# Squared-ReLU attention and a gated feed-forward layer: the third batch's keys and queries by DMA transposes, with four feed-forward units in front of its attention

## The chip, the core and the metric

The kernel runs on one core of a Trainium2 chip. The metric is the device time of one execution in microseconds (us). Three runs of the kernel before gave 439.3, 439.08 and 439.69 us, median 439.3 us.

The engines are called as the profile calls them: PE (TensorE, matmuls), with its weight loads as PEld; DVE (VectorE); ACT (ScalarE); POOL (GpSimd), which here issues the loads; and SP (SyncE), which here issues the stores and the DMA transposes. SPq is SP's queue of DMA issues.

## The reference

There are 8 batches of 448 tokens with 12 heads of 64 columns (768 columns in all). The attention has no softmax. The feed-forward layer has 1536 hidden columns.

```python
def _attn_ref(q, k, v):                        # each (8, 12, 448, 64)
    scale = 1.0 / np.sqrt(q.shape[-1])
    scores = scale * np.matmul(q, k.transpose(0, 1, 3, 2))
    attn = np.maximum(scores, 0.0) ** 2 / S
    return np.matmul(attn, v)

def _moe_ref(x, w_gate, w_val, w_out):         # x is the attention's output as (3584, 768)
    gate = np.maximum(x @ w_gate, 0.0)
    val = x @ w_val
    return gate * val @ w_out
```

Inputs and output are float32. The kernel computes in bf16, sums in float32, and applies all the scales at the end, when it copies the output from PSUM.

## The kernel before, in words

**Order.** Every instruction is pinned, so each engine runs its own instructions in the order in which the code issues them, and waits in place for what the others have not finished. Batches are numbered b = 0 to 7. Batch 0 has its own loop (`first_batch`). Batches 1 to 7 run in `batch(b)`, which goes through n = 0 to 7. At each n it issues three score or value tiles (`burst`), then ACT's ReLU (line 166) and DVE's square (line 170) of the scores, and one or two "gaps". A gap takes units of the feed-forward layer of the batch before from the list `ffn` and issues them. So while batch b's attention runs, batch b - 1's feed-forward layer fills PE.

**Units.** A `gv_unit` makes one 128-row block of the gate and of the value product: 12 matmuls each, an ACT ReLU for the gate, and a DVE multiplication into `hT` (line 244). An `out_unit` makes 384 output columns for 128 tokens with 24 matmuls, and an ACT copy (line 267); the second half's unit issues two stores of 192 KB on SP (line 275). Batches come in pairs: an even batch brings 12 gv units and 6 out units, an odd one 12 and 8. `start_gaps` spreads the units that are left in `ffn` evenly over the gaps of a batch.

**Keys and queries.** Scores need keys and queries with the head's 64 columns on the partitions (`operands`, line 142). There are two ways. For batches below `PE_B` (line 126), `transposes` makes 16 PE transposes for one pair of heads into a PSUM tile `kq_ps` (line 159), and DVE copies it to `kq_sb` (line 161). These run in the middle of a unit (`midway`), one pair of heads at a time, and the next batch's first pair is made at n = 6. From `PE_B` on, `dma_transposes(b)` is called at n = 2 of the batch before: DVE copies the keys into `kr` and the queries into `qr`, regrouped (line 136), and SP issues four DMA transposes for `kT` and four for `qT` (line 139). Each of the four covers a quarter of the tokens for all heads, so the first score tile of a batch needs the first `kT` transpose and all four `qT` transposes. `kr` and `qr` exist once.

**Loads.** POOL issues `kn`, `qn` and `vn` (line 90), two DMAs each, for batch b + 1 at n = 0 of batch b. There are two buffers of each, so a load waits until the last reader of the buffer is done, and all loads behind it on POOL wait too. The readers of `kn` and `qn` are PE's transposes in one way and DVE's regrouping copies in the other. `low_values(b)` (line 108) is a small DVE copy inside `vn`, needed before batch b's first value tile at n = 2. It is issued at n = 5 of the batch before, and for batch 1 at that batch's head.

**Value tiles.** Every eighth tile of a batch is a value tile: `av_last` opens it in the burst, `av_rest` closes it after the first gap, and DVE copies it into `xT` (line 416). Three of these copies complete `xT` of a batch, at n = 2, 5 and 7, and the batch's feed-forward units read it.

Of the kernel before, what the change touches and what calls it, by code (L numbers as in the profile page):

```python
# [16 lines left out]
def kernel(  # L17
# [17 lines left out]
    B, H, S, D = q.shape  # L35
# [24 lines left out]
    def pin(ins):  # L60
        return tc.keep_in_program_order(ins)
# [36 lines left out]
    def load_qk(b, h0=0, h1=H):  # L98
        load_nat(kn_b[b % NB], k, b, h0, h1)
        load_nat(qn_b[b % NB], q, b, h0, h1)  # L100

    def load_v(b):
        load_nat(v_b[b % NB], v, b, 0, H)

    def low_values(b):

        t = v_b[b % NB].rearrange("p (q s h) i d -> p q s h i d", s=2, h=2)
        pin(nc.vector.tensor_copy(t[64:128, :, 1, :, 3, :], t[0:64, :, 1, :, 3, :]))
# [14 lines left out]
            dma_in(wo_sb[c], rows.rearrange("(kf p) m -> p kf m", p=128))  # L123


    PE_B = 3
    kr = const.tile([128, 4, d_model], BF16, name="kr")
    qr = const.tile([128, 4, d_model], BF16, name="qr")
    kT_b = [const.tile([128, HP, 512], BF16, name=f"kT{i}") for i in range(NB)]
# [1 line left out]
    def dma_transposes(b):  # L131

        n = b % NB
        for nat, grp, tr in ((kn_b[n], kr, kT_b[n]), (qn_b[n], qr, qT_b[n])):
            o = grp.rearrange("p i (h d) -> p i h d", d=D)
            pin(nc.vector.tensor_copy(o, nat.rearrange("p h i d -> p i h d")))
            for i in range(4):
                r = 128 if i < 3 else 64
                pin(nc.sync.dma_start_transpose(out=tr[:, :, i * 128:i * 128 + r], in_=grp[0:r, i, :]))


    def operands(b, hp):

        if b >= PE_B:
            n = b % NB
# [23 lines left out]
    def square_part(dst, r):  # L169
        pin(nc.vector.tensor_tensor(dst, r, r, ALU.mult))  # L170

    def relu2(src, dst, n):
        square_part(dst, relu_part(src, n))
# [25 lines left out]
    def av_rest(b, qd, attn, banks):  # L199
        for c in range(2):  # L200
            for i in range(3):
                for h2, o in HALVES:
                    mm(banks[c][o, :], v_b[b % NB][:, 4 * qd + 2 * c + h2, i, :], attn[:, 8 * c + 2 * i + h2, :], False, i == 2)
# [16 lines left out]
    def flush_relu():  # L220
        while late:
            src, dst, n = late.pop(0)
            late_squares.append((dst, relu_part(src, n)))

    def flush():
        flush_relu()
        while late_squares:
            square_part(*late_squares.pop(0))
# [50 lines left out]
    def ffn_units(b):  # L279
        b0 = b - b % 2  # L280
        if b == b0:
            hT_of[b0] = hpool.tile([128, KF, 2 * S], BF16, name="hT")
        hT, xT = hT_of[b0], xT_of[b]
        units = [lambda mf=mf: gv_unit(b, mf, xT, hT) for mf in range(KF)]
        for t in (range(0, 3) if b == b0 else range(3, 7)):
            cuts = [0, OH, OH + OH // 2, d_model] if b == B - 1 and t == 6 else [0, OH, d_model]
            for c0, c1 in zip(cuts, cuts[1:]):
                units.append(lambda t=t, c0=c0, c1=c1: out_unit(b0, t, c0, c1, hT, o_state))
        return units


    ffn = []
    share = [0, 0, 0]

    def start_gaps(of):
        share[:] = [len(ffn), of, 0]

    def gap():

        n, of, i = share  # L300
        for _ in range((i + 1) * n // of - i * n // of):
            ffn.pop(0)()
        flush()
        share[2] = i + 1
# [22 lines left out]
    def transpose_pair(b, hp):  # L327
        kqs[b, hp] = operands(b, hp)

    def attn_of(b, qd):  # L330
        if (b, qd) not in attns:
            attns[b, qd] = atpool.tile([128, 14, S], BF16, name="attn")
        return attns[b, qd]

    def burst(b, tiles):

        todo, begun = [], None
        for qd, kind, c, i in tiles:
            attn = attn_of(b, qd)
            if kind == "pair":  # L340
                todo.append(scores(kqs[b, 2 * qd + c], i, attn, 8 * c + 2 * i))
            elif kind == "last":
                todo.append(scores_last((kqs[b, 2 * qd], kqs[b, 2 * qd + 1]), attn))
            else:
                ps = sc_tile()
                banks = [ps[:, c, :S] for c in range(2)]
                av_last(b, qd, attn, banks)
                begun = (qd, banks, ps[:, :, :S])
        return todo, begun

    def first_batch():
        banks = [av_bank(), av_bank()]
        idle_matmuls(banks[0], 14)
        transpose_pair(0, 0)
        idle_matmuls(banks[0], 4)
        av_at = {4: 0, 5: 1, 6: 2}
        for n in range(len(tiles_first) // 3):
            todo, _ = burst(0, tiles_first[3 * n:3 * n + 3])
            if n in av_at:
                av_last(0, av_at[n], attn_of(0, av_at[n]), banks)  # L360
            relu2(*todo[0])
            if n not in av_at:
                idle_matmuls(banks[0], 2)
            if n + 1 < HP:
                transpose_pair(0, n + 1)
            if n not in av_at:
                idle_matmuls(banks[0], 1)
            relu2(*todo[1])
            relu2(*todo[2])
            if n == 3:  # L370
                low_values(0)
            if n in av_at:
                qd = av_at[n]
                av_rest(0, qd, attn_of(0, qd), banks)
                for c in range(2):
                    x = xT_of[0][:, 2 * qd + c, :]
                    if (qd, c) == (NQ - 1, 0):
                        pin(nc.scalar.activation(x, banks[c], AF.Copy))
                    else:
                        pin(nc.vector.tensor_copy(x, banks[c]))  # L380
                banks = [av_bank(), av_bank()] if qd + 1 < NQ else None
# [3 lines left out]
    PAIR_AT = {0: 1, 1: 2, 2: 3, 3: 4, 5: 5, 6: 6}  # L385

    def batch(b):
        if b == 1:
            low_values(1)
        gaps = [(1, 1)] * 8  # L390
        if b == 1:
            gaps = [(0, 1), (1, 1), (1, 1), (0, 1), (0, 1), (0, 1), (0, 1), (1, 1)]
        elif b == 2:
            gaps[5] = (0, 2)
        start_gaps(sum(map(sum, gaps)))
        pending = None
        for n in range(len(tiles_later) // 3):
            todo, begun = burst(b, tiles_later[3 * n:3 * n + 3])
            relu2(*todo[0])
            relu2(*todo[1])  # L400
            late.extend(todo[2:])
            if n == 0 and b < B - 1:
                load_qk(b + 1)
                load_v(b + 1)
            if n in PAIR_AT:
                hp = PAIR_AT[n]
                if hp < HP:
                    midway.append(lambda hp=hp: transpose_pair(b, hp))
                elif b + 1 < B:
                    midway.append(lambda: transpose_pair(b + 1, 0))  # L410
            for _ in range(gaps[n][0]):
                gap()
            if begun:
                qd, banks, both = begun
                av_rest(b, qd, attn_of(b, qd), banks)
                pin(nc.vector.tensor_copy(xT_of[b][:, 2 * qd:2 * qd + 2, :], both))  # L416
            if b + 1 < B and n == 2 and b + 1 >= PE_B:
                dma_transposes(b + 1)
            if b + 1 < B and n == 5:
                low_values(b + 1)  # L420
            for _ in range(gaps[n][1]):
                gap()

    for b in range(B):
        xT_of[b] = xpool.tile([128, KD, S], BF16, name="xT")
        if b == 0:
            first_batch()
        else:
            batch(b)
        if b + 1 < B:  # L430
            ffn.extend(ffn_units(b))
            if b == 0:
                for _ in range(6):
                    ffn.pop(0)()
                midway.append(lambda: transpose_pair(1, 0))
                ffn.pop(0)()
    flush()
    while ffn:
        ffn.pop(0)()
# [31 lines left out]
```

## Time and profile before

| What | Value |
|---|---|
| Median of three runs | 439.3 us |
| The profiled execution's own time | 438.88 us |
| Its span in the trace | 437.0 us |
| PE busy | 425.9 us, 97% of the span |
| DVE, ACT, POOL busy | 210.3, 217.3, 51.9 us |
| Granted PE clock | 1.00 |
| Moved by DMA | 42.22 MB, mean 97 GB/s |

The page has these parts: busy time of each engine; the span in 40 slices with the busy tenths, the DMA share and GB/s; the DMA queues; the chain of work that ended last; groups of instructions with their mean duration and the idle time before them; and DMA issues with the time to landing. The trace behind it gives single instructions in order of time. Batch b's attention begins with its first burst; these stand at 45.93 us for batch 1, 82.94 for batch 2, 137.92 for batch 3, 186.76 for batch 4, 239.51 for batch 5, 288.56 for batch 6 and 341.31 for batch 7.

The loads of a batch are 384 + 288 KB each for keys, queries and values in the units of the page. A DMA share above 1 means that the 16 DMA engines had more than one packet under way.

### The profile page before, as it was taken

Reading aid. Unit: us, or ns where it says so; the run is one execution under the profiler, and the core shown is the slowest. Engines: PE = TensorE matmul, PEld = TensorE weight load, DVE = VectorE, ACT = ScalarE, POOL = GpSimd, SP = SyncE. Lnnn points to the kernel's source line nnn. Section 1 sums busy time; section 2 is a strip of 40 time slices with the busy share of each in tenths; the row PEclk is TensorE's granted clock in tenths of the full one; section 3 lists DMA queues with packets and bytes.
Section 4 is the critical chain, followed back from the end, with each engine's and each line's share of the span. In section 5 each row is a group of like instructions: output and inputs, shape, how many; then the busy total and the mean of one; then the engine's idle time right before and its main releaser. Section 6 shows DMA issues by size and latency. Waiting matters only on the chain.

```text
span 437.0 us, 11447 instructions
## 1 busy us (share of the span) xinstructions
PE 425.9 (97%) x5076; PEld 251.2 (57%) x5076; DVE 210.3 (48%) x332; ACT 217.3 (50%) x323; POOL 51.9 (12%) x75
## 2 busy tenths in 40 slices
PE   7889999999999999999999999999999999999996
PEld 3447655556566555655566555655566555566664
DVE  3872766547534565345533575435653354522210
ACT  3952647554545544564544655545455645532221
POOL 8624302100024000120003000010000000000001
PEclk9999999999999999999999999999999999999999
DMA  9999999912299951393715923170323200030014
GB/s 107 187 204 195 203 205 202 185 40 63 66 152 164 149 84 45 77 190 41 121 38 102 198 65 67 38 137 1 83 47 87 60 2 1 6 102 4 1 38 108
DMA packets 80081, 42.22 MB, mean 97 GB/s; under 512 B 48640, under 2 KB 76544, under 8 KB 80032
## 3 DMA queue, kind: packets, MB, share of 16 engines
q0 software_dynamic: 47232, 23.70, 41.4%
q1 hardware_dynamic: 32720, 17.75, 16.7%
q8 instruction: 39, 0.64, 0.6%
q14 instruction: 10, 0.08, 0.1%
q10 hardware_dynamic: 80, 0.05, 0.0%
HBM read 47.19 MB, written 11.01 MB: 133 GB/s over the span
## 4 chain that ended last, share of the span: by engine, by line
PE 88%; DMA 6%; DVE 3%; ACT 2%; issue 1%; POOL 1%; POOLq 0%; DVEq 0%; ACTq 0%
PE g_ps L64 25%; PE v_ps L64 24%; PE o_ps L64 24%; PE sc_ps L64 13%; DMA vn<-in_v_dram 5%; PE kq_ps L159 1%; ACT r_sb L166 1%; DVE attn L170 1%; DMA qn<-in_q_dram 1%; DVE kq_sb L161 1%; PE xT_ps L64 0%; POOL kn L90 0%; DVE xT L380 0%; DVE hT L244 0%; POOL qn L90 0%
## 5 line engine op out<-in xcount | busy, mean ns | idle before, releaser
L166 ACT ACTIVATE r_sb<-sc_ps 128x896 bf16<-128x896 f32 x168 | 145.3, 922 | 42.3 <-PE sc_ps L64 42.3
L170 DVE TENSOR_TENSOR attn<-r_sb 128x896 bf16<-128x896 bf16 x168 | 104.2, 623 | 91.1 <-ACT r_sb L166 91.0
L64 PE MATMUL g_ps<-xT,wg 128*64 128x448 bf16 x1152 | 126.0, 354 | 0.0
L64 PE MATMUL v_ps<-xT,wv 128*64 128x448 bf16 x1152 | 125.2, 352 | 0.0
L64 PE MATMUL o_ps<-wo,hT 128*64 128x384 bf16 (+1 forms) x1368 | 115.8, 324 | 0.0
L244 DVE TENSOR_TENSOR hT<-v_ps,g_sb 128x448 bf16<-128x448 f32 x96 | 59.9, 624 | 93.4 <-PE v_ps L64 93.4
L238 ACT ACTIVATE g_sb<-g_ps 128x448 bf16<-128x448 f32 x96 | 52.3, 545 | 92.7 <-PE g_ps L64 92.7
L64 PEld LDWEIGHTS <-hT 128*64 128x64 bf16 x1368 | 75.1, 110 | 37.6 <-issue 6.4
L64 PEld LDWEIGHTS <-wg 128*64 128x64 bf16 x1152 | 63.4, 110 | 49.9 <-issue 12.9
L64 PEld LDWEIGHTS <-wv 128*64 128x64 bf16 x1152 | 66.3, 110 | 41.2 <-issue 0.3
L267 ACT ACTIVATE o_sb<-o_ps 128x384 f32<-128x384 f32 (+1 forms) x57 | 27.9, 489 | 80.5 <-PE o_ps L64 80.5
L64 PE MATMUL sc_ps<-attn,vn 128*64 128x448 bf16 (+1 forms) x336 | 35.1, 354 | 0.0
L90 POOL DMA_DIRECT2D vn<-in_v_dram x16 | 12.1, 769 | 160.3 <-PE sc_ps L64 154.6
L416 DVE CAST xT<-sc_ps 128x896 bf16<-128x896 f32 x21 | 22.9, 1091 | 14.3 <-PE sc_ps L64 14.3
L64 PEld LDWEIGHTS <-vn 128*64 128x64 bf16 (+1 forms) x384 | 19.3, 109 | 18.0 <-issue 5.4
L64 PE MATMUL sc_ps<-qT,kT 64*64 64x448 bf16 x420 | 28.4, 357 | 0.0
L90 POOL DMA_DIRECT2D kn<-in_k_dram x20 | 14.6, 745 | 60.5 <-PE kq_ps L159 55.7
L64 PE MATMUL sc_ps<-kq_sb 64*64 64x448 bf16 x252 | 18.0, 358 | 2.5 <-ACT r_sb L166 1.2
L275 POOL DMA_DIRECT2D out_dram<-o_sb x2 | 1.1, 554 | 146.2 <-ACT o_sb L267 146.2
L64 PEld LDWEIGHTS <-kT 64*64 64x64 bf16 x420 | 9.6, 105 | 14.3 <-issue 11.7
L90 POOL DMA_DIRECT2D qn<-in_q_dram x20 | 14.5, 753 | 4.9 <-DMA wv<-in_moe_w_val_dram 2.2
L161 DVE COPY kq_sb<-kq_ps 128x960 bf16<-128x960 bf16 x18 | 11.8, 654 | 6.3 <-PE kq_ps L159 5.8
(26 smaller groups left out, 81.3 us busy)
## 6 DMA issues: line engine op xcount, KB each, us to landing
out_dram<-o_sb SPq DMA_DIRECT2D x54, 192.0 KB, 2.7
vn<-in_v_dram POOLq DMA_DIRECT2D x8, 384.0 KB, 6.0
kn<-in_k_dram POOLq DMA_DIRECT2D x7, 384.0 KB, 9.0
qn<-in_q_dram POOLq DMA_DIRECT2D x7, 384.0 KB, 11.7
vn<-in_v_dram POOLq DMA_DIRECT2D x8, 288.0 KB, 7.6
wo<-in_moe_w_out_dram POOLq DMA_DIRECT2D x2, 1152.0 KB, 20.9
kn<-in_k_dram POOLq DMA_DIRECT2D x7, 288.0 KB, 10.5
qn<-in_q_dram POOLq DMA_DIRECT2D x7, 288.0 KB, 12.6
```

Source lines behind the costliest of these rows:

```text
L64: pin(nc.tensor.matmul(o, lhsT=l, rhs=r, start=start, stop=stop, skip_group_check=True))
L90: pin(nc.gpsimd.dma_start(out=o, in_=i))
L159: pin(nc.tensor.transpose(o, t[:, 2 * hp + h2, i, :], ident))
L161: pin(nc.vector.tensor_copy(kq, ps[:, 0:512 + S]))
L166: pin(nc.scalar.activation(r, src, AF.Relu))
L170: pin(nc.vector.tensor_tensor(dst, r, r, ALU.mult))
L238: pin(nc.scalar.activation(g_sb, g_ps, AF.Relu))
L244: pin(nc.vector.tensor_tensor(hT[:, mf, col:col + S], v_ps, g_sb, ALU.mult))
L267: pin(nc.scalar.activation(out=o_sb[:, c0:c1], in_=o_ps, func=AF.Copy, scale=float(out_scale)))
L275: pin(e.dma_start(out=segment_rows(b0, 2 * t + s)[:, m], in_=o_sb[s * 64:s * 64 + 64, m]))
L416: pin(nc.vector.tensor_copy(xT_of[b][:, 2 * qd:2 * qd + 2, :], both))
```

## The change

`PE_B` goes from 3 to 2, so batch 2 (the third) takes its keys and queries from DMA transposes, and no PE transposes are made for it. The regrouping copies and the eight transposes for batch 2 are issued at n = 7 of batch 1, after the last `xT` copy and before the last gap, and not at n = 2 as for the later batches. `low_values(b)` moves into batch b itself, at n = 1, for all batches from 1 on. After batch 1 four units of its own feed-forward layer, all gv units, are issued ahead of batch 2's first burst; the 16 units that are left then fall on batch 2's 16 gaps, where 20 did before. The extra gap at n = 5 of batch 2 becomes an ordinary one (the number of gaps is 16 in both).

```diff
-    PE_B = 3
+    PE_B = 2
...
     def batch(b):
-        if b == 1:
-            low_values(1)
         gaps = [(1, 1)] * 8
         if b == 1:
             gaps = [(0, 1), (1, 1), (1, 1), (0, 1), (0, 1), (0, 1), (0, 1), (1, 1)]
-        elif b == 2:
-            gaps[5] = (0, 2)
         start_gaps(sum(map(sum, gaps)))
...
             late.extend(todo[2:])
+            if n == 1:
+                low_values(b)
             if n == 0 and b < B - 1:
                 load_qk(b + 1)
                 load_v(b + 1)
...
-            if b + 1 < B and n == 2 and b + 1 >= PE_B:
+            if b + 1 < B and n == (7 if b == 1 else 2):
                 dma_transposes(b + 1)
-            if b + 1 < B and n == 5:
-                low_values(b + 1)
             for _ in range(gaps[n][1]):
                 gap()
...
                 midway.append(lambda: transpose_pair(1, 0))
                 ffn.pop(0)()
+            if b == 1:
+                for _ in range(4):
+                    ffn.pop(0)()
     flush()
```

## The prediction

> **What bounds the kernel now.** I read the page first: busy times, then the chain that ended last.
>
> ```profile
> span 437.0 us, 11447 instructions
> PE 425.9 (97%) x5076; PEld 251.2 (57%) x5076; DVE 210.3 (48%) x332; ACT 217.3 (50%) x323; POOL 51.9 (12%) x75
> PE 88%; DMA 6%; DVE 3%; ACT 2%; issue 1%; POOL 1%; POOLq 0%; DVEq 0%; ACTq 0%
> ```
>
> PE is the bound in every stage after the start, and it runs in order: PE work taken away shortens the end by its own length, and a PE wait lengthens it by its own. So I looked next at PE's waits after 46 us. There is one of any size, and the timeline shows it in batch 1 at n = 6:
>
> ```profile
> 72.50 0.56 PE L64 MATMUL sc_ps<-kq_sb 64*64 64x448 bf16 x5
> 73.05 0.28 DVE L108 COPY vn<-vn 64x384 bf16<-64x384 bf16 x1 [0.88 <-DMA vn<-in_v_dram]
> 73.36 0.66 DVE L161 COPY kq_sb<-kq_ps 128x960 bf16<-128x960 bf16 x1
> 74.08 0.57 PE L64 MATMUL sc_ps<-kq_sb 64*64 64x448 bf16 x7 [1.01 <-DVE kq_sb L161]
> ```
>
> DVE stood at `low_values(2)` until batch 2's values had landed; the copy that PE needed was queued behind it.
>
> Then the place to which the transposes move, and how they run today for batch 3:
>
> ```profile
> 81.10 1.09 DVE L416 CAST xT<-sc_ps 128x896 bf16<-128x896 f32 x1 [1.13 <-PE sc_ps L64]
> 81.38 1.50 POOL L90 DMA_DIRECT2D vn<-in_v_dram  x2 [6.72 <-PE sc_ps L64]
> 82.94 0.76 PE L64 MATMUL sc_ps<-kq_sb 64*64 64x448 bf16 x12
> ...
> 102.59 0.95 DVE L136 COPY kr<-kn 128x3072 bf16<-128x3072 bf16 x1
> 103.57 5.27 SPq L139 DMA_TRANSPOSE kT<-kr  x4
> 108.95 5.18 SPq L139 DMA_TRANSPOSE qT<-qr  x4
> ...
> 120.68 1.50 POOL L90 DMA_DIRECT2D kn<-in_k_dram  x2 [37.81 <-PE kq_ps L159]
> ```
>
> The 82.94 line is batch 2's first burst. Batch 3's transposes were issued from 103.57 to 114.13 us and were needed only at 137.92. The last line is the load of batch 4's keys: POOL was held until batch 2's PE transposes had read the buffer.
>
> **Removed: PE transposes of batch 2.** Six pairs of heads. Batches 2, 4 and 6 each hold 20 units and the same bursts; batch 2 lasts 82.94 to 137.92 = 54.98 us, batches 4 and 6 last 52.75 (186.76 to 239.51, 288.56 to 341.31). The 2.23 us are five pairs (the first is made in batch 1), 0.446 each. Six: **-2.7 us**, all on PE. The six DVE copies of 0.65 us go too; DVE is off the path.
>
> **Moved: `low_values`.** Without the wait at 72.16 to 73.05 the `kq_sb` copy follows the `xT` copy, ending at 72.16 + 0.66 = 72.8, and PE goes on at about 72.9 instead of 74.08: **-1.2 us**. At n = 1 of batch 2 the values have long landed (73.0). In the other batches its 0.28 us waited for nothing, before the move and after.
>
> **Added: regrouping and the wait.** I follow the clock of the trace of before. PE reaches the end of batch 1 earlier by 1.2 and one pair of transposes (0.45), so the `xT` copy ends at 82.19 - 1.65 = 80.5, the `kr` copy (0.95) at 81.5, `qr` at 82.4. The next DVE work is the first gv unit's product, about 83.6, so the copies cost PE nothing; uncovered they would cost 1.9. SP's first transpose is issued at 81.5. Quiet, from first issue to last landing (last issue plus 2.6) the five batches took 11.9, 12.8, 12.7, 12.3 and 13.0 us. Median 12.7: landing at 94.2; best, 93.4.
>
> PE comes to the place of the old burst at 82.94 - 1.65 = 81.3. Four gv units at 2.27 us (first gate matmuls at 31.73 and 34.01 in the row of units at the start) carry it to 90.4. The units are only moved, so they add no work. The first burst needs all of `qT` and waits in order with nothing behind it that PE could take: **+3.8 us even if the transposes run as quietly as today**, +3.0 at the best pace. That alone eats the 3.9 gained.
>
> **But they do not run quietly.** Today no load is under way beside a transpose. In the new place, `vn` for batch 3 is issued at about 79.7, and batch 4's `kn` and `qn`, which waited until 120.68, now wait only for the regrouping copies: issued from 81.5 to about 85. That is 2.0 MB. Nothing shows transposes beside loads, so I bound it. Nearest row: the stores, which go through the same queue, alone and beside just such a group of six loads:
>
> ```profile
> out_dram<-o_sb SPq DMA_DIRECT2D x2, 192.0 KB, 2.6
> ...
> qn<-in_q_dram POOLq DMA_DIRECT2D x1, 384.0 KB, 11.7
> out_dram<-o_sb SPq DMA_DIRECT2D x2, 192.0 KB, 6.3
> ```
>
> (The first from 225 to 227 us, the others from 186 to 200.) A store beside loads lands 3.7 us later. And the work itself, in the table of stretches (columns: stretch, its length, each engine's busy time, clock, DMA share, GB/s):
>
> ```profile
> 104.00:109.00 5.00, 5.00 (x72) 3.05 (x66) 3.92 (x7) 3.46 (x5) 0.00 (x0) 1.00 0.55 123
> 109.00:115.00 6.00, 6.00 (x72) 3.25 (x68) 2.50 (x4) 3.36 (x6) 0.00 (x0) 1.00 0.57 129
> 195.00:199.00 4.00, 4.00 (x46) 2.42 (x44) 1.78 (x3) 1.35 (x3) 0.00 (x0) 1.00 1.33 168
> ```
>
> The eight transposes keep the DMA engines 5 x 0.55 + 6 x 0.57 = 6.2 us. Six loads at the 195 GB/s or so of the loaded slices take 10.3, from 82.2 on, when the loads before them end: 92.5. If the two shared without any gain from overlap, both end at 98.7. So the last landing lies between 93.4 and 98.7, with another 1 us above for single issues of 2.3 to 2.45 us instead of 1.25, as three batches had. The last transpose is issued at about 92.2 and lands quietly at 94.2 (median pace); with the store's whole 3.7 it would be 97.9, but by then the loads thin out. I take 2.2 of it: 96.4. Wait: **+6.0 us**, ends 3.0 and 9.3.
>
> The Trainium skill bears on this (DMA: Bandwidth & Descriptors, "Queues, rings and completion order"): each DMA engine serves the queues that have work in turn, a packet at a time, so loads and transposes would share and neither would be shut out. By that rule I would estimate a landing of 97.5 and a sum of 444.3 in place of 443.2; the store's 3.7 us agree in sign, and no run here shows the transposes' share.
>
> **PE after the wait.** The wait may cost more than its length. At the start PE came from idle:
>
> ```profile
> 1.16 4.67 PE L64 MATMUL xT_ps<-blank 128*64 128x448 bf16 x28 [1.16 <-DVE blank L74]
> 31.73 1.33 PE L64 MATMUL g_ps<-xT,wg 128*64 128x448 bf16 x12
> ```
>
> Twelve such matmuls take 1.14 from start to start when PE has been busy, so 28 should take 27 x 0.095 + 0.36 = 2.9; they took 4.67, 1.8 more, though the granted clock reads 1.00. After the 1.0 us wait at 73 the next unit shows no loss. So the ends are 0 and 1.8; a wait of 6 us is more like the idle start than like 1.0: **+1.8**.
>
> The Trainium skill has a rule that speaks against this change (TensorE: Matmul & The Clock Gate, "Part 1: The HAM clock gate"): after an idle window of about 3.4 us PE runs at half clock until a busy one has passed. The start's 1.8 us agree with it; no wait in the trace is long enough to show it in mid-run. By the rule the sum is 443.2, by the 1.0 us wait's row 441.4.
>
> **The sum.** -2.7 - 1.2 + 6.0 + 1.8 = +3.9 on 438.88 (span 437.0 and 1.9 around it) = 442.8; the profile is 0.4 below the median, so 443.2 in medians.
>
> Other queues: on SP the eight transposes stand ahead of the two stores of batch 1's last out unit (83.57 today, then about 93); their buffer is one of three and is wanted again late in batch 2. Values for batch 4 still wait on POOL for the end of batch 2. With two units between bursts instead of 2.5, ACT has three ReLUs and two copies, 3 x 0.9 + 2 x 0.5 = 3.7 us, against 4.6 of PE; batch 1 managed with one unit. Zero for these; if that cover failed, a few tenths for each of seven steps.
>
> **Rivals.**
> Cover holds (other side): loads do not disturb the transposes and the pace is the best of five, 11.9. The wait is 3.0, too short to slow PE: -0.9, 438.4. It decides at a landing of 93.4, below which the kernel is faster by more than 0.2% (0.9 us, about what a measurement here can tell). For: DMA engines had idle half of the time in the transposes' stretches. Against: four of five paces are slower, and all six loads fall there. 0.07.
> Quiet at the median pace: wait 3.0 to 4.8, 438.4 to 440.2, say 439.2. 0.12.
> PE's clock stays up: as forecast without 1.8: 441.4. For: the granted clock never left 1.00 in any row. Against: the start. 0.22.
> Starved: the loads go first and the transposes end last, 98.7 to 99.7, wait 8.8: 446.0. For: a store's data waited 3.7 us. Against: loaded slices reached 327 GB/s where stores ran beside loads at 190, so the two overlapped. 0.17.
> That the transposes replace nothing is excluded: batch 2's PE transposes are gone from PE's order.
>
> **How the numbers follow.** The forecast, 443.2, has 0.42 (its own range 441.5 to 445). Faster 0.07, same 0.12, slower 0.22 + 0.42 + 0.17 = 0.81. Range 439.0 to 446.8: it leaves out the faster case, and the far end of the starved one.
>
> **What would show it.** A PE wait on `qT` before batch 2's first burst, 4 to 8 us, beginning about 90.4; no wait at 73; transposes issued from 81.5 with landings above 4 us each; `kn` and `qn` loads near 82; the first unit after the wait slower than 2.27 us. It is wrong if the burst starts before 93.4, or if a new wait appears inside batch 2.

## The result and the profile after

The changed kernel takes 452.0 us (median of four executions, 450.64 to 452.74) against 439.19 for the kernel before: a ratio of 1.0285, with a 95% interval of 1.0261 to 1.0309. It is 2.9% slower. The forecast was 443.2 us with a range to 446.8. The direction was right; the size was three times too small, and the time lies outside the range.

The page of the changed kernel, its busy times and its chain:

```profile
span 449.9 us, 11267 instructions
PE 425.4 (95%) x4980; PEld 249.4 (55%) x4980; DVE 208.9 (46%) x328; ACT 217.4 (48%) x323; POOL 52.8 (12%) x75
PE 88%; SPq 4%; DVE 3%; DMA 2%; ACT 1%; issue 1%; POOL 1%; POOLq 0%; DVEq 0%; ACTq 0%
```

PE is still the bound, but SP's queue, which was nowhere in the chain before, now holds 4% of it. PE's waits after 46 us (engine, line, what it waited for: total, times, longest) are a single line:

```profile
PE sc_ps L64 <- DMA qT<-qr: 15.2, 1, 15.2
```

The wait in batch 1 on the `kq_sb` copy has gone, as forecast. In its place stands one wait for `qT`, 15.2 us long. The timeline shows what led to it:

```profile
80.42 0.95 DVE L136 COPY kr<-kn 128x3072 bf16<-128x3072 bf16 x1
81.40 10.19 SPq L139 DMA_TRANSPOSE kT<-kr  x4
81.73 1.88 POOL L90 DMA_DIRECT2D kn<-in_k_dram  x2
83.59 1.51 POOL L90 DMA_DIRECT2D qn<-in_q_dram  x2
91.70 10.44 SPq L139 DMA_TRANSPOSE qT<-qr  x4
105.56 1.33 PE L64 MATMUL sc_ps<-qT,kT 64*64 64x448 bf16 x12 [15.16 <-DMA qT<-qr]
106.83 2.31 PE L64 MATMUL g_ps<-xT,wg 128*64 128x448 bf16 x12
108.98 1.30 PE L64 MATMUL v_ps<-xT,wv 128*64 128x448 bf16 x12
```

The start is as forecast: the transposes go out at 81.4 us and the loads of batch 4's keys and queries at 81.7. But four transposes take SP 10.2 and 10.4 us to issue, where they took 5.3 and 5.2. The last issue and what PE waited for stand in the chain (start, us, what):

```profile
94.53 2.88 SPq L139
97.45 2.74 SPq L139
100.24 5.19 DMA qT<-qr
```

The last landed at 105.4 (issue at 100.2, 5.2 to landing), 24.0 us after the first issue; in the profile of before this took 11.9 to 13.0.

The PE lines behind the wait are slow too. From burst to unit takes 1.27 us where 0.69 is usual, and the first twelve matmuls of the unit take 2.15 where 1.16 is: 1.6 us in all. The table of stretches has the clock (columns: stretch, its length, busy time of PE, PEld, DVE, ACT, POOL, then granted clock, DMA share, GB/s):

```profile
92.00:96.00 4.00, 0.00 (x0) 0.00 (x0) 0.00 (x0) 0.00 (x0) 0.00 (x0) 0.90 1.38 180
96.00:100.00 4.00, 0.00 (x0) 0.00 (x0) 0.00 (x0) 0.00 (x0) 0.00 (x0) 0.50 1.38 181
104.00:108.00 4.00, 2.44 (x20) 1.03 (x22) 0.67 (x2) 1.73 (x2) 0.00 (x0) 0.50 0.49 142
112.00:116.00 4.00, 4.00 (x48) 2.10 (x46) 2.42 (x5) 2.98 (x5) 0.00 (x0) 1.00 0.02 4
```

The clock is halved during the wait and stays so until some 3 us of work are done. Together, with the two gains as they were forecast: -2.7 (transposes) - 1.2 (the wait in batch 1) + 15.2 + 1.6 = 12.9 us, and the spans differ by 449.9 - 437.0 = 12.9. So nothing else of size is needed to explain the difference. What is left to explain is why eight transposes took 24 us.

### The profile page after: what moved, and what is told of

Same layout as the page of the kernel before. It is cut to its first block, busy times and chain, and to the rows that moved or that the text cites. A ratio compares the mean times of both kernels' runs of the same rounds, so it can differ in the third digit from the quotient of the medians.

```text
span 449.9 us, 11267 instructions
## 1 busy us (share of the span) xinstructions
PE 425.4 (95%) x4980; PEld 249.4 (55%) x4980; DVE 208.9 (46%) x328; ACT 217.4 (48%) x323; POOL 52.8 (12%) x75
## 3 DMA queue, kind: packets, MB, share of 16 engines
q1 hardware_dynamic: 38352, 19.13, 19.7%
## 4 chain that ended last, share of the span: by engine, by line
PE 88%; SPq 4%; DVE 3%; DMA 2%; ACT 1%; issue 1%; POOL 1%; POOLq 0%; DVEq 0%; ACTq 0%
PE g_ps L64 24%; PE o_ps L64 24%; PE v_ps L64 23%; PE sc_ps L64 14%; SPq L139 4%; ACT r_sb L166 1%; PE kq_ps L159 1%; DMA qT<-qr 1%; DVE attn L170 1%; DMA qn<-in_q_dram 1%; DVE kq_sb L161 1%; PE xT_ps L64 0%; POOL kn L90 0%; DVE qr L136 0%; DVE xT L380 0%
## 5 line engine op out<-in xcount | busy, mean ns | idle before, releaser
L64 PE MATMUL sc_ps<-qT,kT 64*64 64x448 bf16 x504 | 34.6, 362 | 15.2 <-DMA qT<-qr 15.2
L64 PEld LDWEIGHTS <-kT 64*64 64x64 bf16 x504 | 11.7, 106 | 32.5 <-issue 29.5
L64 PEld LDWEIGHTS <-vn 128*64 128x64 bf16 (+1 forms) x384 | 19.4, 109 | 17.6 <-issue 5.0
L64 PE MATMUL sc_ps<-kq_sb 64*64 64x448 bf16 x168 | 12.0, 358 | 1.5 <-ACT r_sb L166 1.2
L64 PE MATMUL xT_ps<-blank 128*64 128x448 bf16 x60 | 10.1, 462 | 1.2 <-DVE blank L74 1.2
```

The lines of the kernel that those rows point to most:

```text
L64: pin(nc.tensor.matmul(o, lhsT=l, rhs=r, start=start, stop=stop, skip_group_check=True))
```

## The experiments

The theory, "loads": the transposes are slow because 2 MB of loads run beside them. Its rival, "place": SP is slow in that place whatever the loads do.

**All loads out of the way.** `hold_loads` keeps batch 3's values, and with them all that stands behind on POOL, until the last transpose has landed. The small write must wait for the transposes that read `qr`; `qr` is written anew before it is next used.

```diff
             if n == 0 and b < B - 1:
                 load_qk(b + 1)
+                if b == 2:
+                    pin(nc.gpsimd.memset(qr[0:1, 3, 0:2], 0.0))
                 load_v(b + 1)
```

> The changed kernel, with batch 3's values and batch 4's keys and queries held on POOL until the last transpose for batch 2 has landed (a two-element POOL memset in qr, which must wait for the transposes that read it, stands ahead of the load of batch 3's values). Theory 'loads': the transposes took 20.6 us of issue and 24 us to the last landing because 2 MB of loads ran beside them. Then they go back to 12 to 13 us, land near 94, PE waits 3.0 to 4.8 us instead of 15.2, and the time is 438.3 to 440.1 us, up to 1.6 more if PE still comes back slow. Rival 'place': SP's issue is slow there for another reason (behind the stores, or the regrouping copies), whatever the loads do. Then the wait stays near 15 and the time near 452.

Measured: 440.7 us (ten executions, 439.86 to 442.23), ratio 1.0028 [1.0007, 1.0049]. The timeline of this kernel:

```profile
81.60 6.69 SPq L139 DMA_TRANSPOSE kT<-kr  x4
88.41 5.17 SPq L139 DMA_TRANSPOSE qT<-qr  x4
94.82 0.09 POOL L403 MEMSET qr<- 1x2 bf16 x1 [19.91 <-DMA qT<-qr]
94.85 1.33 PE L64 MATMUL sc_ps<-qT,kT 64*64 64x448 bf16 x12 [4.25 <-DMA qT<-qr]
96.11 2.45 PE L64 MATMUL g_ps<-xT,wg 128*64 128x448 bf16 x12
98.35 2.41 PE L64 MATMUL v_ps<-xT,wv 128*64 128x448 bf16 x12
100.59 1.30 PE L64 MATMUL g_ps<-xT,wg 128*64 128x448 bf16 x12
```

In the same place, with the same issue order on SP, the transposes take 11.9 us of issue and land 13.2 us after the first issue. "Place" falls; the loads cost 11 of the 15.2 us. The `kT` half is still a little slow (6.69), because one of its four issues took 2.7 us, from 84.3 to 87.0. Loads were not beside that one: batch 3's keys and queries had landed by about 84, and from 85.0 to 86.5 hardly anything moved at all (22 packets of SP's queue, none of POOL's). The kernel before has single issues of 2.3 to 2.45 us too, with no load under way. What makes such a pause stays open. The wait of 4.2 us is the one that four units leave open even in quiet.

**A third of the loads.** `hold_kq` lets batch 3's values run beside the transposes and delays only batch 4's keys and queries:

```diff
             if n == 0 and b < B - 1:
-                load_qk(b + 1)
-                load_v(b + 1)
+                if b == 3:
+                    load_v(b + 1)
+                    load_qk(b + 1)
+                else:
+                    load_qk(b + 1)
+                    load_v(b + 1)
```

> The changed kernel, with batch 4's values loaded ahead of its keys and queries, so that the keys and queries stand on POOL behind a wait for batch 2's end. Only batch 3's values (a third of the 2 MB) are left beside the transposes. Theory 'loads': a wait in between, since the values take some 4 to 6 us of the window: last landing near 97, wait 5 to 8 us, 441 to 445 us. Rival 'place': no change, near 452.

Measured: 444.69 us, ratio 1.012 [1.0091, 1.0149]. PE's wait in this kernel:

```profile
PE sc_ps L64 <- DMA qT<-qr: 6.6, 1, 6.6
```

And SP's issues in its timeline:

```profile
81.72 8.99 SPq L139 DMA_TRANSPOSE kT<-kr  x4
90.83 5.18 SPq L139 DMA_TRANSPOSE qT<-qr  x4
```

The wait grows with what runs beside the transposes: 4.2 us with all six loads held, 6.6 with 672 KB left, 15.2 with 2016 KB. Only the `kT` half, which meets the values, is slow; the `qT` half keeps the quiet 5.2.

**How the two share.** The packet counts of the queues say more than the times. q0 carries POOL's loads, q1 SP's transposes (columns: packets, MB, share of 16 engines). In the changed kernel from 84 to 86 us, from 95 to 98, from 98 to 100 and from 102 to 104:

```profile
q0 software_dynamic: 722, 0.32, 136.7%
q1 hardware_dynamic: 9, 0.00, 0.9%
...
q0 software_dynamic: 767, 0.36, 88.4%
q1 hardware_dynamic: 765, 0.19, 48.4%
...
q0 software_dynamic: 541, 0.23, 87.8%
q1 hardware_dynamic: 541, 0.13, 50.9%
...
q1 hardware_dynamic: 885, 0.22, 131.4%
q0 software_dynamic: 54, 0.02, 7.8%
```

And in the kernel before, loads alone (146 to 148 us) and transposes alone (104 to 114 us):

```profile
q0 software_dynamic: 807, 0.39, 146.1%
...
q1 hardware_dynamic: 5216, 1.28, 56.6%
```

The eight transposes are 5632 packets (q1 has 38352 in the page after, 32720 before), the six loads 768 each, 4608 in all. The transposes' 24.0 us have three parts.

- *A late start.* From 82.5 to 85.5 us the loads moved 990 packets and the transposes none, although SP had issued the first at 81.4. In `hold_loads`, where it was issued at 81.6, q1 moved 1299 packets from 82.5 to 85.
- *Equal counts.* From 91.6 to 100 the two queues move the same number, 2180 and 2174. Loads alone run at 404 packets per us and transposes at 522, gaps between issues included; together each gets about 260. So they share by packets, not by bytes, and a transpose's packets are small: 0.19 MB in 765, against 0.36 MB in 767. Whether they alternate one by one the counts can't say.
- *The rest.* At 100 us all but some 480 of the loads' packets had gone, but only about 3160 of the transposes' 5632. The others took until 104.9, at some 500 per us.

Between the first two parts lies a stretch in which neither queue got on: from 88.0 to 91.6 us the loads moved 495 packets and the transposes 408. So the equal turns are shown for 8.4 of the 24.0 us; what sets the late start and the slow stretch stays open.

The slow issue on SP is probably a consequence. POOL had issued its last load at 85.1 us, and SP still needed 2.3 to 3.6 us per transpose up to 100; while the engines were behind, the queue would take new transposes only as old ones went through. That the queue fills up is inferred, not shown by a run.

**The rest of the change, without the transposes.** `no_transposes` keeps `low_values` at its new place, the four units and the even gaps:

```diff
-    PE_B = 2
+    PE_B = 3
...
-            if b + 1 < B and n == (7 if b == 1 else 2):
+            if b + 1 < B and n == 2 and b + 1 >= PE_B:
                 dma_transposes(b + 1)
```

> The changed kernel with PE_B back at 3 and the DMA transposes for later batches at n = 2 as before: what is left of the change is low_values at n = 1 of its own batch, the four units in front of batch 2 and its 16 even gaps. Both theories: the PE wait in batch 1 is gone and nothing else changes, 1.2 us faster than before, 438.0 us. If the four units or the even gaps cost something in batch 2, it shows here as a time above 438.

Measured: 437.81 us, ratio 0.9969 [0.9955, 0.9982], with no PE wait after 46 us and a span 1.2 us shorter than before (435.8 against 437.0). So this part of the change is a gain of the size that the timeline had shown, and no cost of the four units shows.

**PE's clock.** Two runs fill the wait with the blank matmuls that the kernel uses at its start, 22 pairs in the held kernel and 72 in the changed one:

```diff
             if b == 1:
                 for _ in range(4):
                     ffn.pop(0)()
+                idle_matmuls(av_bank(), 22)      # hold_warm; 72 in warm
```

> As hold_loads, with 22 pairs of blank matmuls (about 4.2 us) behind the four units. Theory 'clock': hold_loads' profile shows a wait of 4.2 us and 2.9 us of slow matmuls after it, and its median (440.7) lies 1.5 above what a wait alone gives, 439.0 - 3.9 + 4.2 = 439.3. With PE kept busy the time is 439.3 and the spread between executions (439.9 to 442.2) shrinks. Rival 'no clock': it stays at 440.7.

Measured: 439.12 us, ten executions from 438.91 to 439.82, so the time fell by 1.6 us and the spread from 2.4 to 0.9, as the clock theory said. The two kernels ran on different chips; as ratios to the kernel before on the same chip they stand at 1.0028 and 0.9983. The mean granted clock goes with the times: it was 0.990 to 0.992 in the four executions of `hold_loads` above 441 us, 0.994 to 0.996 in the other six, and 0.998 to 1.000 in all ten of `hold_warm`. The lines behind the blank matmuls:

```profile
90.34 4.33 PE L64 MATMUL xT_ps<-blank 128*64 128x448 bf16 x44
94.59 0.76 PE L64 MATMUL sc_ps<-qT,kT 64*64 64x448 bf16 x12
95.29 1.32 PE L64 MATMUL g_ps<-xT,wg 128*64 128x448 bf16 x12
```

The same burst and unit, with the same operands fresh from the transposes, run at full pace. That the first use of the operands makes them slow is excluded.

> The changed kernel with 72 pairs of blank matmuls (about 13.7 us, as at the kernel's start) behind the four units, where PE would stand still for 15.2 us. They cost no time as long as they end before qT lands. Theory 'clock': the burst and the first unit after the wait were 1.6 us slower in the changed kernel's profile because PE had been idle; with blank matmuls in the wait they run at full pace and the time falls from 452.0 to about 450.4. Rival 'no clock': what comes after the wait is slow for another reason (first use of the new operands), and the time stays at 452.

Measured: 450.83 us, ratio 1.025 [1.0218, 1.0283]. It lies where the clock theory put it, but the interval overlaps that of the changed kernel, so by times alone this run is inconclusive. Its profile has the 12 gate matmuls after the wait at 1.15 us again instead of 2.15, and a span of 447.9 against 449.9:

```profile
105.22 0.76 PE L64 MATMUL sc_ps<-qT,kT 64*64 64x448 bf16 x12 [1.45 <-DMA qT<-qr]
105.91 1.33 PE L64 MATMUL g_ps<-xT,wg 128*64 128x448 bf16 x12
107.06 1.30 PE L64 MATMUL v_ps<-xT,wv 128*64 128x448 bf16 x12
```

**Enough cover.** `hold_six` is `hold_loads` with two more units in front:

```diff
             if b == 1:
-                for _ in range(4):
+                for _ in range(6):
                     ffn.pop(0)()
```

> As hold_loads, with six units in front of batch 2 instead of four: PE has 4.5 us more to do before it needs qT. Theory 'loads': PE comes to the first burst near 94.9, the transposes have landed at 94.2, no wait and no slow PE: -2.7 - 1.2 = -3.9, 435.3 us, faster than both. Rival 'place': a wait of some 10.7 us is left, 447.

Measured: 435.11 us (435.01 to 435.53), ratio 0.9902 [0.9881, 0.9922]: 1% faster than the kernel before. It has no PE wait after 46 us, and its span, 433.2, is 3.8 below that of before. In the timeline the last unit runs into the burst, and the loads have only been moved behind the transposes:

```profile
93.77 1.30 PE L64 MATMUL v_ps<-xT,wv 128*64 128x448 bf16 x12
94.29 0.09 POOL L403 MEMSET qr<- 1x2 bf16 x1 [19.45 <-DMA qT<-qr]
95.00 0.76 PE L64 MATMUL sc_ps<-qT,kT 64*64 64x448 bf16 x12
```

**Cover alone.** `eleven` leaves the loads where the change put them and hides the slow transposes behind eleven units:

```diff
             if b == 1:
-                for _ in range(4):
+                for _ in range(11):
                     ffn.pop(0)()
```

> The changed kernel with eleven units in front of batch 2 instead of four, and the loads left beside the transposes as they are. PE then has 25.0 us to do from 81.3, to 106.3, and qT landed at 105.4. If the wait and what follows from it are all that the loads cost, there is no wait and the time is 439.0 - 3.9 = 435.1, as in hold_six. If fewer units left over for batch 2's 16 gaps (9 for 16) uncover ACT or DVE there, it is slower than that, 436 to 438.

Measured: 436.7 us, ratio 0.9928 [0.9905, 0.995]. The transposes are as slow as in the changed kernel (10.07 and 11.42 us of issue), PE waits for them only 0.2 us, and the kernel is faster than before. PE's waits after 46 us:

```profile
PE sc_ps L64 <- DVE xT L414: 0.7, 1, 0.7
PE sc_ps L64 <- DMA qT<-qr: 0.2, 1, 0.2
```

It is 1.6 us behind `hold_six`, which ran on another chip, and in the two profiles all of that arises by the end of batch 2: batch 3's first burst stands at 135.69 us against 134.13. One wait inside batch 2 is named, 0.7 us of PE for DVE's `xT` copy; the remainder is spread in small pieces that I did not take apart. That nine units for sixteen gaps leave the bursts too close together is my reading, not shown by a run.

## Why the prediction was wrong

**Removed transposes, -2.7, and the wait in batch 1, -1.2: right.** `no_transposes` shows 1.2 in its span, and `hold_six`, which has both and no wait, 3.8 for the two together.

**The cover of four units, to 90.4: right.** The units ended near 90.4 in the changed kernel, and the first issue fell at 81.4 where 81.5 was forecast. The quiet wait of 3.8 was 4.2 in `hold_loads`. So it held that this wait alone eats the 3.9 gained: with the loads out of the way the kernel takes 440.7 us, no less than before.

**The last landing, "between 93.4 and 98.7" and "I take 2.2 of it: 96.4": wrong, and this is the whole miss.** It was 105.4, so the wait was 15.2 us in place of 6.0. The step that failed is the pace of SP's issue. The prediction had the last transpose "issued at about 92.2", at the quiet pace, and put the loads' whole effect into one late landing, 4.2 us after that. It was issued at 100.2, 8.0 us later, and landed 5.2 after. In `hold_loads`, without the loads, the last issue is at 92.3 and the landing at 94.8.

The point came from a store beside loads, 3.7 us late, and that row shows only the late start. In the kernel before, that store was issued at 187.39, and q1 moved nothing up to 191.3, 3.9 us later, where the quiet pair at 225.68 had its first packet after 1.1; then both stores went through in under 2.7 us. A store of 192 KB is 80 packets (the trace of before counts 160 packets and 0.39 MB for two of them), a transpose 704 on average, of about a quarter of a KB. So the row could show what the start costs, but not what it costs to share the engines for thousands of packets.

The upper bound failed too. It added the engine time of both kinds of work, each as it runs alone: 10.3 us for the loads (10.6, as the page's KB are of 1024 bytes) and 6.2 for the transposes. Counting packets would hardly have moved it: 4608 / 404 + 5632 / 914 us (704 packets in the 0.77 us of engine time that the prediction had for a transpose) are 11.4 + 6.2 = 17.6 us, from 82.2 to 99.8. The other 5.6 us are time in which the engines did less than that. By the same two rates, which makes this an estimate, the packets from 88.0 to 91.6 us were worth 1.7 of the 3.6 us, and those from 102 to 104 1.1 of the 2; the rest is in smaller pieces. The prediction had allowed 1 us for stretches of this kind, from single issues of 2.3 to 2.45 us in the kernel before. Why they arise is open.

The Trainium skill's rule that the prediction cited (DMA: Bandwidth & Descriptors, "Queues, rings and completion order"), that each engine serves its queues in turn by packets, is what the counts 767 and 765 agree with, if the packets of the profile are those that the page means, which no run here shows. The 9 against 722 before them do not look like turns.

**PE after the wait, +1.8: right in kind and size.** It was 1.6 in the changed kernel's profile, and `hold_warm` shows the cause. That the size fits is partly luck: the same piece cost 2.8 us behind the shorter wait of `hold_loads` and 1.9 behind that of `hold_kq`. The rival "PE's clock stays up" falls.

**The rivals.** "Starved" (446.0) was nearest in size, and right in part: the loads moved alone at first, were nine tenths done at 100 us, and the transposes ended last. Against it, the two queues shared evenly from 91.6 to 100, and its wait of 8.8 us was 6.4 too short. "Cover holds" and "quiet" fail for the changed kernel; with the loads held and two more units the first comes true.

## What to carry to other kernels

Before a transfer is moved, look which other transfers its new place releases: here the regrouping copies freed the buffers that had held POOL back until 120 us, so the move itself brought the loads beside the transposes. For two queues side by side, count packets and not only bytes: while both had work here, small packets ran at the pace of the pair. And take the sum of the engine times as the least that it costs, not as the most: here it gave a landing at 99.8 us, and the landing was at 105.4. A wait of PE of 4.2 us or more cost, in these runs, its length and a slow stretch behind it; more work in front of it, or even blank matmuls, take the second part away.

## What the runs showed of the hardware

Eight DMA transposes of 5632 packets took 11.9 to 13.2 us from first issue to last landing with none of the six loads beside them, and 24.0 us beside all six. Total traffic beside each other was only about 180 GB/s, where bursts of transposes alone reach 290 and loads alone some 195.

A shorter wait did not cost less afterwards. The wait of 4.2 us in `hold_loads` was followed by 2.8 us of loss in its profile (three slow pieces, full pace 5.7 us after the restart), the 15.2 us wait by 1.6 (full pace after 3.4 us). The Trainium skill (TensorE: Matmul & The Clock Gate, "Part 1: The HAM clock gate") says that the window in which activity is judged runs freely, so that the loss depends on where in it the work restarts; the two profiles agree with that, and so does the spread of `hold_loads`, 2.4 us between executions where the same kernel with blank matmuls has 0.9. No run varies the place of the restart alone.

A queue can start late beside another's loads. In the changed kernel the transposes moved almost nothing from 84 to 86 us, 9 packets against 722 of the loads, before the counts became even, and a pair of stores in the kernel before stood still for 3.9 us behind its issue. In `hold_loads` POOL's queue still had the last of batch 3's keys and queries to move (242 packets from 82.5 to 85 us), and the transposes started all the same. What sets the order there stays open.
